# Alpha's transposes of the first nine units in the dense products' banks and one unit earlier

## The chip, the cores and the metric

The kernel runs on one core of a Trainium2 chip. The time is the device time of one execution in microseconds (us). Five engines each work through a queue of their own: TensorE (PE: matrix products, and transposes as products with an identity), VectorE (DVE), ScalarE (ACT), GpSimd (POOL) and SyncE (SP, which here issues the DMAs). An engine that meets an instruction whose input isn't ready waits, and all that is queued behind it waits too.

## What is computed

Gated linear attention, then a feed-forward layer on its output:

```python
state = np.zeros((B, H, D, D))                       # B=4, H=8, S=768, D=48
for t in range(S):
    state = alpha[:, :, t, :, None] * state + einsum('bhd,bhe->bhde', k[:, :, t], v[:, :, t])
    y[:, :, t] = einsum('bhd,bhde->bhe', q[:, :, t], state)
x = y.transpose(0, 2, 1, 3).reshape(B * S, H * D)    # 3072 x 384
h = x @ w_in                                         # 384 x 2048
out = np.maximum(0.01 * h, h) @ w_out                # 2048 x 384
```

## The kernel before

The 768 tokens of each batch are cut into chunks of 128, which gives 24 units (chunk t, batch b) of 128 tokens and 8 heads; heads go in four pairs p. Unit numbers run over the batches first, so units 0 to 3 are the first chunk of the four batches, 4 to 7 the second.

For a unit u the running products of alpha along the tokens turn the recurrence into products of matrices. `scans(u)` transposes alpha so that tokens lie along the free axis (four transposes on PE, L303) and then forms on DVE `pc`, the running product of each pair (four scans), and `rc`, its inverse counted backwards. `scaled_q` and `scaled_k` transpose q and k on PE and multiply them on DVE by `pc` and `rc`; the results are `qs` and `ks` (DVE writes them at L288, as it does `pc`, `rc` and the low half of y). Then:

- `scores(u)` multiplies `qs` by `ks` on PE (16 products into two banks, L540). `mask_scores` copies them on ACT to `sm` (L420) and zeroes a triangle on POOL (L422).
- `k_tokens(u)` transposes `ks` back (L437, tile `kt`), and ACT copies it to `ktok`.
- `past(u)` multiplies `qs` by the state into the bank of y, `values(u)` adds the masked scores times v to it, and `products(u)` makes the new part of the state, `kv`, from `ktok` and v. All three are L540 in the profile.
- `split(u)` writes y as a high half (ACT, L554) and a low half (DVE, tile `large`); `next_state(u)` adds `kv` to the state.

The first nine units (`AHEAD`) are issued by `attention(0, 9)`, in which unit u+1 is prepared while unit u is multiplied. Later units transpose on DVE and are spread among the dense products. The dense layer has 16 blocks f of 128 columns. The weights of a block come by DMA (tile `raw`) and `convert(f)` splits them into high and low parts on ACT (L260, L262, L269) and DVE (L266, L273, L275, L277, L280; tiles `bits`, `pw`, `w`). `ffn_in` multiplies into a bank `ph` (L714, nine products). ACT and DVE then form `t` (L719, L722), `gh` (L724) and `gl` (L728). `ffn_out` multiplies these by the second weights (L743). Two early `ffn_in` are placed behind `kt` of units 7 and 8 (`STARTS`).

PSUM has eight banks: two of tag `ph`, three of tag `a`, three of tag `b`. Within a tag the banks go round, so a new tile waits for the readers of the tile that had its bank. In the first nine units `bank()` gives `a` and `b` in turn. So alpha's, q's and k's transposes, both score banks, `kt`, y and `kv` all share one rotation. Unit 0's alpha goes half to `a` and half to `ph`.

Loads: q, k and alpha each have two buffers, with three more shared ones (`spare`), v has three. A load is issued on SP when the code asks for it, and waits for the buffer's last reader.

The order of an engine's instructions is not simply the order of the code. The compiler's scheduler places the instructions by its own estimate of times, within the dependencies, the pools' rotations and the explicit `behind(...)` marks, which hold an instruction behind a named earlier one. So a change in the first part moves rows on every engine. Lines on which the prediction turns:

```python
BEGIN = ("rc", 7), ("qs", 8), ("kt", 8)
STARTS = {62: ("kt", 7), 69: ("kt", 8)}
...
with behind("ks", u):
    convert(converted)
```

Of the kernel before, what the change touches and what calls it, by code (L numbers as in the profile page):

```python
# [10 lines left out]
F32 = mybir.dt.float32  # L11
# [13 lines left out]
def gated_linear_attn_ffn(ctx, tc, q, k, v, alpha, w_in, w_out, out):  # L25
    nc = tc.nc
    B, H, S, D = q.shape
    NT, DM = out.shape
    DF = w_in.shape[1]
    P = 128  # L30
# [3 lines left out]
    NP = H // 2  # L34
# [37 lines left out]

    halves = slice(0, HC), slice(HC, C)

    kinds = ["a", "b"]

    def bank(tag=None):
        if tag is None:
            tag = kinds[0]
            kinds.append(kinds.pop(0))  # L80
        return ps_x.tile([P, 512], F32, name=tag)

    def pieces(name, dtype, *shapes):
# [99 lines left out]
        if n < NV - 1:  # L183
            load_values(n)

    idle = ps_h.tile([P, 512], F32, name="ph")

    def keep_warm(n):

# [97 lines left out]

        return put(u >= AHEAD, "DVE", lambda: op(*args))  # L288

    def banks4():  # L290
        return bank().rearrange("r (p n) -> r p n", p=NP)

    def transposed(u, i, name, **kw):

        src = loaded(u, i)
        if u < AHEAD:
            ps = banks4()
            tiles = [ps[:, p, :] for p in range(NP)]
            if u == 0 and i == 0:
                other = ps_h.tile([P, 512], F32, name="ph").rearrange("r (p n) -> r p n", p=NP)  # L300
                tiles[NP // 2:] = [other[:, p, :] for p in range(NP // 2)]
            for p in range(NP):
                last = nc.tensor.transpose(  # L303
                    tiles[p], by_token(src)[:, 2 * p:2 * p + 2, :].rearrange("t h d -> t (h d)"), ident
                )
                if u == 0 and p % 2:
                    with tc.issue_after(last.ins):
                        keep_warm(WARM[2 * i + p // 2])
            return [ps, other] if u == 0 and i == 0 else ps
        t = atp.tile([P, NP, C], F32, name=name, **kw)  # L310
        src = src.rearrange("r (p n) -> r p n", p=NP)[:, :, 0:RUN]
        vector(
            u, nc.vector.transpose, t.rearrange("r p (j t) -> r p t j", t=T4),
            src.rearrange("r p (t d) -> r p t d", t=T4)[:, :, :, 0:32],
        )
        return t
# [114 lines left out]
    def k_tokens(u):  # L431
        if u >= AHEAD or units[u][0] < NC - 1:
            ks = live[u][2]
            kt = bank()
            for p in range(NP):
                with in_row() if u >= AHEAD else nullcontext():
                    made["kt", u] = nc.tensor.transpose(kt[:, p * BR:(p + 1) * BR], ks[0:BR, p, :], ident[0:BR, 0:BR])  # L437
            if row and u >= AHEAD:
                row[:] = [made["kt", u]]
            ktok = atp.tile([P, NP, BR], F32, name="ktok", bufs=1)  # L440
            made["sm", u] = nc.scalar.copy(ktok.rearrange("t p d -> t (p d)"), kt[:, 0:NP * BR])  # L441
            live[u][2:] = [ktok] if u < AHEAD else [ks, ktok]
# [10 lines left out]
    def past(u):  # L453

        tb, b = units[u]
        qs, W = live[u][1], state[b].rearrange("r p n -> r (p n)")
        y = banks4()
        ys[u] = [y]
        if tb:
            for q, s, lo, top, p, at in heads():  # L460
                c, m = p * BR + lo, D if top else HB
                yield y[at:at + m, 2 * q + s, :], W[0:BR, c:c + m], qs[0:BR, p, :], q == 0 and s == 0, False
# [33 lines left out]
    def products(u):  # L496

        tb, b = units[u]
        pe, qs, ktok = live[u][:3]
        V = vals_sb[u % NV]  # L500
        kv = None
        if tb < NC - 1:
            kv = bank()[:, 0:NP * D].rearrange("d (p e) -> d p e", p=NP)
            for p in range(NP):
                for s, lo, m in ((0, 0, HB), (1, HB, D)):
                    h = 2 * p + s
                    yield kv[lo:lo + m, p, :], ktok[:, p, lo:lo + m], V[:, h * D:(h + 1) * D], True, True
        load_values(u + NV)
        live[u] = pe, kv
# [99 lines left out]
    def every_step(steps):  # L609

        for _ in steps:
            pass

    def attention(first, last):

        for u in range(first - 1, last):
            new, old = u + 1 < last, u >= first
            if new:
                every_step(scans(u + 1))
                yield  # L620
            if old:
                multiply([scores(u)])
                yield
                mask_scores(u)
                yield
                k_tokens(u)
                sum_up(u)
                yield
            if new:
                every_step(scaled_q(u + 1))  # L630
                yield
                every_step(scaled_k(u + 1))
                yield
            if old:
                multiply([past(u), values(u), products(u)])
                split(u)
                yield
                next_state(u)
                if u % UPB == UPB - 1:
                    gather(u // UPB)  # L640
                    ready.add(u // UPB)
                yield
# [140 lines left out]
    for n, _ in enumerate(st):  # L783
# [12 lines left out]
        if n in STARTS:  # L796
            i, f = items[len(gs)][:2]
            with behind(*STARTS[n]):
                gs[len(gs)] = ffn_in(i, f)
    kinds[:] = "a"  # L800


    new = coming = None
# [197 lines left out]
```

## Time and profile before

| what | value |
|---|---|
| time, median of 3 runs | 511.39 us (510.27 to 513.04) |
| profiled execution, its own time | 510.39 us |
| span of that execution | 508.7 us |
| granted TensorE clock, mean | 0.997 |
| PE busy | 496.5 us (98%) |
| DVE busy | 371.3 us (73%) |
| ACT busy | 250.4 us (49%) |
| POOL busy | 68.7 us (13%) |
| DMA | 46.77 MB |

The profiled execution lies 1.00 us below the median of the runs, and 1.7 us of it are outside the span. Times in rows of the profile count from the span's start. In a row of the timeline stand the start, the duration, the engine, the line, what is written from what, the number of instructions, and in square brackets the engine's idle time just before, with what ended it. PE's matrix products overlap each other, so a row's duration is not the engine's pace.

### The profile page before, as it was taken

What the parts mean: (1) busy time and instruction counts of PE and PEld (TensorE: products, weight loads), DVE (VectorE), ACT (ScalarE), POOL (GpSimd) and SP (SyncE); (2) the same over time, 40 slices, a digit from 0 to 9 for tenths busy, and PEclk for the clock granted to TensorE, in tenths of its full rate; (3) what the DMA queues carried; (4) which work ended last, traced back from release to release, by engine and by line L of the source; (5) the groups of instructions that cost most, each with busy time, mean ns of one, the idle gap of its engine ahead of it and who ended that gap; (6) DMA issues with size and microseconds to landing.
All of it is one profiled execution on the core that took longest, in us unless ns stands there. A gap on an engine that the chain in (4) does not pass through costs nothing.

```text
span 508.7 us, 12195 instructions
## 1 busy us (share of the span) xinstructions
PE 496.5 (98%) x4906; PEld 479.1 (94%) x4906; DVE 371.3 (73%) x700; ACT 250.4 (49%) x524; POOL 68.7 (13%) x161
## 2 busy tenths in 40 slices
PE   8998999999999999999999999999999999999995
PEld 7786899999999999999999999999999999999995
DVE  7999899999999768777768578676768674333331
ACT  2666877767655444454444453354444543333331
POOL 5554500000001111101201211101101100000000
PEclk9999999999999999999999999999999999999998
DMA  9999986777204423524325323324321101001001
GB/s 145 167 184 182 220 179 181 208 170 204 36 1 118 139 62 73 120 60 120 73 59 115 102 60 90 70 68 118 78 57 40 50 2 24 1 0 48 1 0 52
DMA packets 92990, 46.77 MB, mean 92 GB/s; under 512 B 57856, under 2 KB 90112, under 8 KB 92928
## 3 DMA queue, kind: packets, MB, share of 16 engines
q1 hardware_dynamic: 92928, 45.93, 40.9%
q8 instruction: 40, 0.66, 0.6%
q14 instruction: 22, 0.18, 0.1%
HBM read 38.83 MB, written 4.72 MB: 86 GB/s over the span
## 4 chain that ended last, share of the span: by engine, by line
PE 80%; DVE 8%; DMA 6%; issue 2%; ACT 2%; SPq 2%; POOL 0%; DVEq 0%; ACTq 0%; POOLq 0%
PE ph L714 34%; PE b L743 32%; PE a L540 5%; PE a L743 3%; DMA raw<-in_moe_w_in_dram 3%; PE ph L540 2%; PE a L437 1%; DMA small<-in_alpha_dram 1%; DMA small<-in_v_dram 1%; DVE gl L728 1%; DVE ks L288 1%; DVE qs L288 1%; SPq L224 1%; DVE pw L277 1%; DVE t L722 1%
## 5 line engine op out<-in xcount | busy, mean ns | idle before, releaser
L714 PE MATMUL ph<-large,w 128*128 128x384 f32 x1152 | 225.1, 336 | 0.4 <-DVE w L280 0.2
L714 PEld LDWEIGHTS ph<-large,w 128*128 128x128 f32 x1152 | 200.5, 188 | 2.1 <-DVE t L722 1.1
L743 PE MATMUL b<-w,gh 128*128 128x384 f32 x672 | 168.3, 337 | 0.0
L722 DVE TENSOR_TENSOR t<-ph,t 128x384 f32<-128x384 f32 x128 | 70.4, 550 | 71.9 <-ACT t L719 71.8
L743 PEld LDWEIGHTS b<-w,gh 128*128 128x128 f32 x672 | 119.9, 188 | 1.3 <-ACT gh L724 0.2
L719 ACT ACTIVATE t<-ph 128x384 f32<-128x384 f32 x128 | 62.6, 489 | 111.5 <-PE ph L714 111.5
L724 ACT CAST gh<-t 128x384 fp32r<-128x384 f32 x128 | 65.8, 514 | 97.1 <-DVE t L722 97.0
L743 PE MATMUL b<-w,gl 128*128 128x384 f32 x336 | 108.1, 334 | 0.0
L728 DVE TENSOR_TENSOR gl<-t,gh 128x384 fp32r<-128x384 f32 x128 | 70.5, 551 | 31.1 <-ACT gh L724 31.1
L743 PEld LDWEIGHTS b<-w,gl 128*128 128x128 f32 x336 | 62.7, 188 | 0.0
L422 POOL TENSOR_SCALAR_AFFINE_SELECT sm<-sm 64x256 f32<-64x256 f32 (+1 forms) x48 | 26.2, 555 | 45.0 <-ACT sm L420 37.9
L288 DVE TENSOR_TENSOR_SCAN down<-e,small 128x511 f32<-128x511 f32 x15 | 19.3, 1287 | 6.4 <-DMA out_dram<-o 5.0
L535 POOL MEMSET small<- 128x1 f32 x15 | 1.5, 99 | 152.7 <-PE a L540 149.8
L540 PE MATMUL a<-qs,ks 48*64 48x64 f32 (+1 forms) x552 | 20.9, 228 | 0.2 <-ACT ktok L441 0.2
L288 DVE TENSOR_TENSOR_SCAN up<-e,small 128x128 f32<-128x128 f32 x60 | 20.4, 403 | 0.1
L743 PE MATMUL a<-w,gh 128*128 128x384 f32 x96 | 20.5, 334 | 0.0
L540 PEld LDWEIGHTS a<-qs,ks 48*64 48x64 f32 (+1 forms) x552 | 17.6, 142 | 1.8 <-issue 1.3
L358 POOL COPY small<-up 128x4 f32<-128x4 f32 x15 | 5.9, 395 | 94.6 <-DVE up L288 94.6
L262 ACT CAST signs<-raw 128x768 f16<-128x768 f32 x16 | 17.2, 1076 | 0.1
L743 PEld LDWEIGHTS a<-w,gh 128*128 128x128 f32 x96 | 17.0, 188 | 0.0
L288 DVE STREAM_TRANSPOSE e<-small 128x512 f32<-128x512 f32 x15 | 16.9, 1126 | 0.0
L420 ACT COPY sm<-a 128x256 f32<-128x256 f32 (+1 forms) x24 | 10.8, 452 | 11.7 <-PE b L540 11.7
(113 smaller groups left out, 612.4 us busy)
## 6 DMA issues: line engine op xcount, KB each, us to landing
raw<-in_moe_w_out_dram SPq DMA_DIRECT2D x16, 384.0 KB, 4.0
small<-in_v_dram SPq DMA_DIRECT2D x24, 192.0 KB, 3.9
raw<-in_moe_w_in_dram SPq DMA_DIRECT2D x32, 144.0 KB, 4.2
out_dram<-o SPq DMA_DIRECT2D x24, 192.0 KB, 2.7
small<-in_alpha_dram SPq DMA_DIRECT2D x32, 96.0 KB, 2.5
small<-in_q_dram SPq DMA_DIRECT2D x30, 96.0 KB, 2.2
small<-in_k_dram SPq DMA_DIRECT2D x30, 96.0 KB, 2.2
small<-in_alpha_dram SPq DMA_DIRECT2D x30, 80.0 KB, 2.2
```

The source lines that it names most:

```text
L262: put(ordered, "ACT", lambda: nc.scalar.copy(signs.bitcast(F16).rearrange("p (n w) -> p n w", w=2)[:, :, 1], top.bitcast(F32)))
L288: return put(u >= AHEAD, "DVE", lambda: op(*args))
L358: nc.gpsimd.tensor_copy(pe, pc[:, :, C - 1:C])
L420: made["sm", u] = nc.scalar.copy(sm[s], ss[s] if u < AHEAD else within(ss[s]))
L422: made["mask", u] = nc.gpsimd.affine_select(out=sm[s][part], in_=sm[s][part], compare_op=ALU.is_ge, fill=0.0, base=0, pattern=[[0, NP], [1 ...
L540: made["product",] = nc.tensor.matmul(out, weights, moving, start=start, stop=stop, skip_group_check=True)
L714: product = nc.tensor.matmul(ph, w_in_of(f, wn, g), xt[:, g, :], start=n == 0, stop=n == 3 * NG - 1)
L719: put(ordered, "ACT", lambda: nc.scalar.mul(t, ph, 0.01))
L722: put(ordered, "DVE", lambda: nc.vector.tensor_tensor(t, ph, t, ALU.max))
L724: put(ordered, "ACT", lambda: nc.scalar.copy(gh, t))
L728: made["gl", i, f] = put(ordered, "DVE", lambda: nc.vector.tensor_tensor(gl, t, gh.bitcast(F32), ALU.subtract))
L743: product = nc.tensor.matmul(po[j], gt[:, js], w_out_of(f, wn), start=f == 0 and n == 0, stop=f == NF - 1 and n == 2)
```

## The change

Alpha's transposes of the first nine units go to the banks of tag `ph`, which only the dense products (and, in unit 0, half of alpha and the idle products that keep PE busy at the start) used. The transposes of q and k and both score banks go to tag `a`; `kt`, y, `kv` and the idle products go to tag `b`. There is no rotation over both tags any more.

The transposing step of `scans` is taken out of its place and issued one unit earlier: `turn_alpha(u + 2)` stands right behind `scaled_k(u + 1)` and ahead of `past(u)`. For u = 4 and 5 two marks hold it there: alpha's transposes of unit u+2 behind the last transpose of k of unit u+1, and the first product of `past(u)` behind alpha's last transpose. The load of alpha is asked for as much earlier. The numbers of the lines shift: L303 becomes L300, L288 L285, L540 L538, L437 L435, L714 L728, L743 L757, L722 L736, L728 L742, L266 to L280 become L263 to L277.

```diff
--- before.py
+++ after.py
@@ -72,12 +72,9 @@
 
     halves = slice(0, HC), slice(HC, C)
 
-    kinds = ["a", "b"]
-
-    def bank(tag=None):
-        if tag is None:
-            tag = kinds[0]
-            kinds.append(kinds.pop(0))
+    def bank(tag="a"):
+        if tag == "ph":
+            return ps_h.tile([P, 512], F32, name=tag)
         return ps_x.tile([P, 512], F32, name=tag)
 
     def pieces(name, dtype, *shapes):
@@ -183,7 +180,7 @@
         if n < NV - 1:
             load_values(n)
 
-    idle = ps_h.tile([P, 512], F32, name="ph")
+    idle = bank("b")
 
     def keep_warm(n):
 
@@ -287,22 +284,23 @@
 
         return put(u >= AHEAD, "DVE", lambda: op(*args))
 
-    def banks4():
-        return bank().rearrange("r (p n) -> r p n", p=NP)
+    def banks4(tag="a"):
+        return bank(tag).rearrange("r (p n) -> r p n", p=NP)
 
     def transposed(u, i, name, **kw):
 
         src = loaded(u, i)
         if u < AHEAD:
-            ps = banks4()
+            ps = banks4("a" if i else "ph")
             tiles = [ps[:, p, :] for p in range(NP)]
             if u == 0 and i == 0:
-                other = ps_h.tile([P, 512], F32, name="ph").rearrange("r (p n) -> r p n", p=NP)
+                other = banks4("ph")
                 tiles[NP // 2:] = [other[:, p, :] for p in range(NP // 2)]
             for p in range(NP):
                 last = nc.tensor.transpose(
                     tiles[p], by_token(src)[:, 2 * p:2 * p + 2, :].rearrange("t h d -> t (h d)"), ident
                 )
+                made["turned", u, i] = last
                 if u == 0 and p % 2:
                     with tc.issue_after(last.ins):
                         keep_warm(WARM[2 * i + p // 2])
@@ -431,7 +429,7 @@
     def k_tokens(u):
         if u >= AHEAD or units[u][0] < NC - 1:
             ks = live[u][2]
-            kt = bank()
+            kt = bank("b" if u < AHEAD else "a")
             for p in range(NP):
                 with in_row() if u >= AHEAD else nullcontext():
                     made["kt", u] = nc.tensor.transpose(kt[:, p * BR:(p + 1) * BR], ks[0:BR, p, :], ident[0:BR, 0:BR])
@@ -454,7 +452,7 @@
 
         tb, b = units[u]
         qs, W = live[u][1], state[b].rearrange("r p n -> r (p n)")
-        y = banks4()
+        y = banks4("b")
         ys[u] = [y]
         if tb:
             for q, s, lo, top, p, at in heads():
@@ -500,7 +498,7 @@
         V = vals_sb[u % NV]
         kv = None
         if tb < NC - 1:
-            kv = bank()[:, 0:NP * D].rearrange("d (p e) -> d p e", p=NP)
+            kv = bank("b")[:, 0:NP * D].rearrange("d (p e) -> d p e", p=NP)
             for p in range(NP):
                 for s, lo, m in ((0, 0, HB), (1, HB, D)):
                     h = 2 * p + s
@@ -613,10 +611,19 @@
 
     def attention(first, last):
 
+        turned = {}
+
+        def turn_alpha(u):
+
+            if u < last:
+                turned[u] = scans(u)
+                next(turned[u])
+
+        turn_alpha(first)
         for u in range(first - 1, last):
             new, old = u + 1 < last, u >= first
             if new:
-                every_step(scans(u + 1))
+                every_step(turned.pop(u + 1))
                 yield
             if old:
                 multiply([scores(u)])
@@ -631,8 +638,15 @@
                 yield
                 every_step(scaled_k(u + 1))
                 yield
+            together = B <= u < last - 3
+            with behind("turned", u + 1, 2) if together else nullcontext():
+                turn_alpha(u + 2)
             if old:
-                multiply([past(u), values(u), products(u)])
+                group = past(u)
+                if together:
+                    with behind("turned", u + 2, 0):
+                        multiply([islice(group, 1)])
+                multiply([group, values(u), products(u)])
                 split(u)
                 yield
                 next_state(u)
@@ -797,7 +811,6 @@
             i, f = items[len(gs)][:2]
             with behind(*STARTS[n]):
                 gs[len(gs)] = ffn_in(i, f)
-    kinds[:] = "a"
 
 
     new = coming = None
```

What moves is seen at three places. The names are the program's tiles with the scheduler's numbers; `small_73` and `spare_74` are large tiles of many parts (q, k, alpha, v, the states), and the same number stands for the same piece of work in both kernels only for `ks`, `qs`, `pc`, `rc`, `sm`, `pw` and `bits`.

PE, end of unit 2's scores. Before: the keys of unit 2, then k (`a_391`) and q (`b_383`) of unit 3, two products of y, and alpha of unit 4 (`b_428`):

```order
L437 MATMUL a_374<-small_73,ks_311 128x112 x4
L303 MATMUL a_391<-small_73 128x128 x4
L303 MATMUL b_383<-small_73 128x128 x4
L540 MATMUL b_399<-sm_365,small_73 64x128
L540 MATMUL b_399<-sm_365,small_73 48x128
L303 MATMUL b_428<-small_73 128x128 x4
L540 MATMUL a_408<-small_73,ktok_379 64x48
```

Now: q (`a_383`), the keys, alpha of unit 4 (`ph_399`) and at once alpha of unit 5 (`ph_489`), then k (`a_391`):

```order
L300 MATMUL a_383<-small_73 128x128
L435 MATMUL b_374<-small_73,ks_311 128x112 x4
L300 MATMUL a_383<-small_73 128x128 x3
L300 MATMUL ph_399<-small_73 128x128 x4
L300 MATMUL ph_489<-small_73,spare_74 128x128 x4
L300 MATMUL a_391<-small_73 128x128 x4
L538 MATMUL b_404<-sm_365,small_73 64x128
L538 MATMUL b_404<-sm_365,small_73 48x128
```

Alpha of unit 4 stands ahead of k of unit 3 and y of unit 2, and alpha of unit 5 has come forward by a whole unit. Alpha of unit 3 likewise stands inside unit 0's y, alpha of unit 8 inside unit 5's.

DVE, the scaled keys of unit 7 (`ks_775`), which `scores(7)` on PE reads. `pw_732`, `bits_727` and `w0_726` are the conversion of weight block 0, `pc_811` the scans of unit 8. Before:

```order
L273 TENSOR_SCALAR pw_732<-bits_727 128x768
L288 TENSOR_TENSOR qs_768<-b_763,pc_715 128x512
L275 TENSOR_TENSOR bits_727<-bits_727,w0_726 128x768
L277 SCALAR_TENSOR_TENSOR pw_732<-raw_334,pw_732 128x768
L288 TENSOR_TENSOR ks_775<-a_770,rc_716 128x512
L288 SCALAR_TENSOR_TENSOR pc_811<-b_806,small_73 128x128 x4
L280 TENSOR_TENSOR w0_726<-pw_732,bits_727 128x768
L575 TENSOR_TENSOR small_73<-us2_424,a_794 112x192
```

Now:

```order
L270 TENSOR_SCALAR pw_732<-bits_727 128x768
L272 TENSOR_TENSOR bits_727<-bits_727,w0_726 128x768
L274 SCALAR_TENSOR_TENSOR pw_732<-raw_339,pw_732 128x768
L285 TENSOR_TENSOR qs_768<-a_763,pc_715 128x512
L285 SCALAR_TENSOR_TENSOR pc_811<-ph_777,small_73 128x128
L277 TENSOR_TENSOR w0_726<-pw_732,bits_727 128x768
L285 SCALAR_TENSOR_TENSOR pc_811<-ph_777,small_73 128x128 x3
L285 TENSOR_TENSOR ks_775<-a_770,rc_716 128x512
L573 TENSOR_TENSOR small_73<-us2_429,b_799 112x192
```

`ks_775` has moved behind the four scans of unit 8 and behind the last step of weight block 0.

DVE, the scaled keys of unit 8 (`ks_888`), which `scores(8)` reads. `t_858` and `gl_863` belong to the first `ffn_in`, `bits_873` to weight block 1. Before:

```order
L288 SCALAR_TENSOR_TENSOR rc_812<-b_806,small_73 128x511
L288 TENSOR_TENSOR ks_888<-a_883,rc_812 128x512
L288 TENSOR_TENSOR qs_870<-b_865,pc_811 128x512
L266 SCALAR_TENSOR_TENSOR bits_873<-raw_510,signs_120 128x768
L722 TENSOR_TENSOR t_858<-ph_848,t_858 128x384
L273 TENSOR_SCALAR pw_878<-bits_873 128x768
```

Now:

```order
L285 SCALAR_TENSOR_TENSOR rc_812<-ph_777,small_73 128x511
L736 TENSOR_TENSOR t_858<-ph_848,t_858 128x384
L285 TENSOR_TENSOR qs_870<-a_865,pc_811 128x512
L263 SCALAR_TENSOR_TENSOR bits_873<-raw_515,signs_120 128x768
L742 TENSOR_TENSOR gl_863<-t_858,gh_861 128x384
L285 TENSOR_TENSOR ks_888<-a_883,rc_812 128x512
L270 TENSOR_SCALAR pw_878<-bits_873 128x768
```

`ks_888` has moved behind `t_858`, `qs_870`, `bits_873` and `gl_863`.

On SP the loads of alpha of units 2 to 8 stand 1 to 10 places earlier among the loads, those of k one to three places later, the four pieces of the first weights of block 0 one place later; v of unit 6 is the 40th load in both orders, and from there on the loads agree.

## The prediction

> **What bounds the kernel now.** I first read busy time by stretches, since the average of a kernel in two parts tells little. The columns are the window, its length, then for PE, its weight loads, DVE, ACT and POOL the busy time and the instructions, the granted clock, the DMA share and the rate.
>
> ```profile
> core 0: us, PE busy (x) PEld busy (x) DVE busy (x) ACT busy (x) POOL busy (x), PEclk, DMA share, GB/s
> 40.00:50.00 10.00, 7.90 (x118) 6.48 (x118) 9.61 (x19) 6.04 (x12) 3.50 (x5) 1.00 1.20 192
> 50.00:60.00 10.00, 9.87 (x120) 8.88 (x120) 9.40 (x17) 8.97 (x20) 4.76 (x7) 1.00 0.98 198
> 60.00:70.00 10.00, 9.77 (x87) 8.61 (x81) 8.16 (x14) 7.51 (x14) 2.38 (x2) 1.00 0.92 227
> 70.00:110.00 40.00, 40.00 (x230) 39.81 (x231) 40.00 (x65) 29.69 (x47) 0.00 (x0) 1.00 0.75 186
> 131.00:151.00 20.00, 19.66 (x111) 18.76 (x110) 19.00 (x31) 11.33 (x20) 1.18 (x1) 1.00 0.00 0
> 151.00:300.00 149.00, 148.37 (x1728) 144.96 (x1728) 114.11 (x222) 68.74 (x160) 19.59 (x47) 1.00 0.37 93
> 300.00:480.00 180.00, 179.78 (x1848) 176.73 (x1847) 108.12 (x212) 74.24 (x166) 13.68 (x38) 1.00 0.18 46
> 480.00:508.70 28.70, 23.20 (x134) 22.88 (x133) 7.80 (x14) 7.00 (x14) 0.00 (x0) 0.94 0.07 23
> ```
>
> From 50 us on PE is the bound: it idles 0.13 in 50 to 60, nothing in 70 to 110, 0.63 in 151 to 300, 0.22 in 300 to 480. Whatever makes PE later after 50 us is paid unless one of these small idles takes it back. Only 40 to 50 us has a real hole, 2.10 us. The waits of the first 70 us (total, number, longest) say for what:
>
> ```profile
> PE b L540 <- DMA small<-in_v_dram: 1.6, 2, 1.4
> DVE pc L288 <- PE b L303: 2.6, 4, 1.0
> ```
>
> The second row is the wait that the moved instructions cause: four times DVE stands, 2.6 us in all, before it can scan alpha, because alpha's transposes are late on PE. PE itself waits little for DVE in these units. Its longest wait is a load. The timeline of PE around it, and one row from unit 1 that is needed below:
>
> ```profile
> 18.35 0.66 PE L303 MATMUL b<-small 128*128 128x128 f32 x4 [0.20 <-DMA small<-in_alpha_dram]
> ...
> 44.55 0.66 PE L303 MATMUL a<-small 128*128 128x128 f32 x4 [0.36 <-DVE small L575]
> ...
> 46.17 0.66 PE L303 MATMUL b<-small,spare 128*128 128x128 f32 x4
> 48.27 0.43 PE L540 MATMUL b<-sm,small 128*64 128x128 f32 x4 [1.44 <-DMA small<-in_v_dram]
> ...
> 49.72 0.37 PE L540 MATMUL a<-qs,ks 48*128 48x128 f32 x1
> ...
> 51.19 1.81 PE L714 MATMUL ph<-large,w 128*128 128x384 f32 x9
> ...
> 54.72 1.39 PE L540 MATMUL b<-sm,small 128*48 128x128 f32 x16
> ...
> 56.48 0.37 PE L540 MATMUL b<-qs,ks 48*128 48x128 f32 x1
> ...
> 61.26 0.43 PE L540 MATMUL a<-sm,small 128*64 128x128 f32 x4
> ...
> 61.96 0.87 PE L540 MATMUL a<-sm,small 128*64 128x128 f32 x12 [0.17 <-POOL sm L422]
> ```
>
> At 46.17 is alpha of unit 8. At 48.27 y of unit 6 starts, 1.44 us late, when v of unit 6 lands. `scores(7)` starts at 49.72, the first dense product at 51.19, `scores(8)` at 56.48, y of unit 8 at 61.26. So the part before 48.27 is paced by the loads, and the part behind it by PE and what feeds it. DVE in the same place, which is where the new order bites:
>
> ```profile
> 43.30 0.93 DVE L266 SCALAR_TENSOR_TENSOR bits<-raw,signs 128x768 int32<-128x768 int32 x1
> ...
> 47.03 1.38 DVE L277 SCALAR_TENSOR_TENSOR pw<-raw,pw 128x768 f32<-128x768 uint32 x1
> 48.33 0.68 DVE L288 TENSOR_TENSOR ks<-a,rc 128x512 f32<-128x512 f32 x1
> 48.93 1.35 DVE L288 TENSOR_TENSOR_SCAN pc<-b,small 128x128 f32<-128x128 f32 x4
> 50.21 0.93 DVE L280 TENSOR_TENSOR w<-pw,bits 128x768 fp32r<-128x768 f32 x1
> 51.06 0.34 DVE L575 TENSOR_TENSOR small<-us,a 112x192 f32<-112x192 f32 x1
> ...
> 53.53 0.69 DVE L288 TENSOR_TENSOR ks<-a,rc 128x512 f32<-128x512 f32 x1
> 54.14 0.68 DVE L288 TENSOR_TENSOR qs<-b,pc 128x512 f32<-128x512 f32 x1
> 54.74 1.25 DVE L266 SCALAR_TENSOR_TENSOR bits<-raw,signs 128x768 int32<-128x768 int32 x1
> 56.45 0.56 DVE L722 TENSOR_TENSOR t<-ph,t 128x384 f32<-128x384 f32 x1 [0.46 <-ACT t L719]
> 56.93 0.55 DVE L273 TENSOR_SCALAR pw<-bits 128x768 int32<-128x768 int32 x1
> ...
> 60.00 0.55 DVE L728 TENSOR_TENSOR gl<-t,gh 128x384 fp32r<-128x384 f32 x1
> ```
>
> The keys of unit 7 are made at 48.33 and those of unit 8 at 53.53, 0.7 and 2.3 us before PE asks for them.
>
> **The change, part by part.**
>
> Earlier transposes of alpha. The number of transposes and their durations stay (0.66 us for four). The 2.6 us of DVE's waits go. I cost this at nothing, gain or loss, because what is next is late for another reason: v of unit 6 is the 40th load before and after, the queue is full, and PE cannot pass 48.27 without it. If instead the loads did move up, the gain is bounded by the wait of 1.44 us on PE and by DVE's 2.6.
>
> Transposes that now wait for their load. Alpha of unit 3 ran at 18.35, just as it landed (0.20 us of wait). It is now the 11th load, not the 13th, but its transposes stand ahead of the rest of y of unit 0 and `scores(1)`, and alpha of unit 5 ahead of k of unit 3. PE will stand there, and behind it y and the scores of the unit. What covers this is the same wait for v of unit 6, 1.44 us, and work moved away from 46.17 (0.66 us), which leaves about 2.1 us of hole. I take nothing; the upper end is 1.0, if the two stalls add to more than the hole.
>
> Three banks a tag in place of one rotation of six. In these units the trace shows PE waiting for no reader of a bank beyond 0.4 us (44.55, a transpose behind a DVE read). I take 0, from -0.4 to +0.4.
>
> The keys of unit 7. They now stand behind the four scans of unit 8 and the last step of weight block 0. By the starts above, the scans take 50.21 - 48.93 = 1.28 and that step 51.06 - 50.21 = 0.85. The keys start at 48.33 + 1.28 + 0.85 = 50.46 and end at 51.1. PE, ready at 49.72, stands 1.4 us in front of `scores(7)`. DVE's sequence from 43.30 hangs on the first weights. Rows of SP, ACT, POOL and DVE that this and the next steps use:
>
> ```profile
> 33.57 3.70 SPq L224 DMA_DIRECT2D raw<-in_moe_w_in_dram  x4
> ...
> 40.84 0.92 ACT L260 ACTIVATE raw<-raw 128x768 f32<-128x768 f32 x1 [1.24 <-DMA raw<-in_moe_w_in_dram]
> ...
> 53.30 0.58 ACT L420 COPY sm<-a 128x512 f32<-128x512 f32 x1
> ...
> 57.48 0.56 ACT L724 CAST gh<-t 128x384 fp32r<-128x384 f32 x1
> ...
> 53.95 1.23 POOL L422 TENSOR_SCALAR_AFFINE_SELECT sm<-sm 128x512 f32<-128x512 f32 x2 [2.04 <-ACT sm L420]
> ...
> 58.60 3.31 POOL L422 TENSOR_SCALAR_AFFINE_SELECT sm<-sm 128x512 f32<-128x512 f32 x2 [2.24 <-ACT sm L420]
> ...
> 133.82 1.28 DVE L288 TENSOR_TENSOR_SCAN down<-e,small 128x511 f32<-128x511 f32 x1 [1.00 <-PE b L743]
> ```
>
> These weights are one place later on SP, and four issues took 3.70, so 0.9 a place: 1.4 to 2.3 us at `scores(7)`. Some 0.3 of it comes back at once: y and `kv` of unit 7 take 56.48 - 54.72 = 1.76 us in all, against 49.72 - 48.27 = 1.45 in unit 6, since ACT copies the scores of unit 7 only at 53.30. That copy doesn't move (scores that start at 51.1 to 52.0 end before 53.2).
>
> The keys of unit 8. They now stand behind `t`, `qs`, `bits` and `gl`. `t` starts at 56.45 as before, since ACT's queue ahead of it doesn't move and the dense product, 1.4 to 2.3 later than 51.19, still ends by 55.3. Then 0.48 (56.93 - 56.45), 0.60 for `qs` (54.74 - 54.14), 0.95 to 1.25 for `bits` (rows at 43.30 and 54.74), 0.55 for `gl` (`gh`, done at 58.04, is no hindrance) and 0.6 to 0.7 for the keys: they are ready at 59.6 to 60.0. `scores(8)` starts then, 3.1 to 3.5 us behind 56.48; this contains the lateness from unit 7. I take 3.3.
>
> y of unit 8. It took 61.96 with a pause for the mask, which ran 3.31 us there against 1.23 for unit 7. With the short mask 0.3 to 0.4 us come back; with the long one nothing. The row alone leaves both; I take 0.3 back, so PE is 3.0 behind at 66 us.
>
> By the Trainium skill, SBUF — State Buffer, section Who interferes with whom, a VectorE instruction with two SBUF inputs and a GpSimd one that reads SBUF block each other for whole instructions. The trace agrees: the 3.31 us run beside such rows (`gl` at 60.00, from `t` and `gh`), the 1.23 us start beside reads of PSUM. By it the mask of unit 8 stays long, as L272 and L274 then follow on DVE, and the sum would be 3.3 here.
>
> What is given back. In 131 to 151, 111 products ran in 20.00 us against 230 in 40.00 at 70 to 110, so 4 too few, at 0.174 us each 0.70 us. DVE stood 1.00 us there for a product at 133.82, and was late with the next weights. Then come 0.63 idle to 300 and 0.22 to 480. A PE that is later meets feeders that are ready, so up to 0.70 + 0.63 + 0.22 = 1.55 us; the lower end is 0, if the feeders are as late. I take all of it, because each is a wait for an engine that has slack otherwise (DVE 108 of 180, ACT 74). The last stretch keeps its order.
>
> Sum: 0 + 0 + 0 + 3.3 - 0.3 - 1.55 = +1.45. Against the profiled execution that is 510.39 + 1.45 = 511.84, and since that execution lies 1.00 below the median of the runs (511.39), I forecast 512.84, in short 512.8.
>
> **The rivals.** A difference of 0.5%, 2.56 us, is about what a measurement of this kernel tells from none.
>
> 1. Nothing is given back, and the mask stays long: 3.5 us at `scores(8)`, 514.9, or 515.9 with the uncovered 1.0 of the transposes. For it: DVE and PE are both full from 70 to 110, so DVE may be as late as PE, and then stands for PE again at 133.82. Against it: DVE has idles of its own in 60 to 70 (8.16 of 10). It decides from 2.56 net, so if less than 0.9 of 3.5 comes back.
>
> 2. Faster: the loads move up. SP waits for a buffer before it issues; with alpha transposed earlier the buffers come free earlier, v of unit 6 lands earlier and the hole of 1.44 and part of DVE's 2.6 go, while the first weights, `t` and `gl` move up by the same and cover the new order of the keys. That gives 1.44 to 2.6 below the time before: 508.8 to 509.9. Against it: DMA shares of 1.20 and 0.98 in 40 to 60 show a queue that is full, not one that waits. It decides if v of unit 6 lands before 46.8, where PE is done with the row at 46.17, and the keys move up as well.
>
> 3. No change: the order written for the engines differs, but the keys are ready as before because DVE, rid of its waits, runs ahead. The chain would then give 511.4, from -0.5 to +0.5. Against it: at 43.30 DVE started on weights that had just come, so it cannot run ahead there.
>
> 4. The clock drops at the hole before y of unit 6. It is 1.44 us now; with alpha of unit 8 taken from 46.17 it is about 2.1. In the last stretch, where PE idles most, the granted clock was 0.94 over 28.7 us, 1.7 us of clock. Such a loss on top gives 512.8 + 1.7 = 514.5. Against it: 40 to 50 us, with 2.10 us idle, kept 1.00.
>
> The Trainium skill, TensorE: Matmul & The Clock Gate, section HAM oscillation — how this bites in real kernels, states that idle gaps above some 3.4 us throttle the clock. The trace agrees so far as its longest quoted gap left the clock at 1.00; by that rule 2.1 us do no harm, which is why this rival has little.
>
> **How the numbers follow.** The forecast (two new waits on PE, a part of them given back, +0.5 to +2.5) has 0.50; rival 1 has 0.25, rival 2 0.10, rival 3 0.10, rival 4 0.05. Rivals 1 and 4 end partly within 2.56, so slower by over 0.5% gets 0.28, faster 0.10, and 0.62 remain for no difference that can be told. The range for 8 in 10 goes from 510.2 (half of rival 2 left out) to 515.1 (the upper end of rival 1 left out); the forecast's own is 511.9 to 513.9.
>
> **What would show it.** Right: PE with a wait of 1 to 2.5 us for DVE's `ks` ahead of each of the two last `scores`; DVE without its four waits for alpha; y of unit 6 still released by v near 48.3; in 131 to 151 more than 111 products. The step of the keys is wrong if `scores(8)` starts before 58 us, the step of the loads if v of unit 6 lands elsewhere than 47.5 to 49, and the part given back if PE's lateness at 66 us is still whole at 480. The prediction as a whole fails if PE stalls for alpha of units 3 and 5 outgrow the hole, or if a bank in a tag of three is waited for.

## The result, and the profile after

The changed kernel took 514.41 us (median of 13 executions, 512.52 to 517.50), the kernel before 512.03 (13 executions, 509.74 to 513.04). The ratio is 1.0065, with a 95% interval from 1.0047 to 1.0083: slower by 0.65%, or 3.3 us. The profiled execution took 514.78 us, its span 513.1, at a mean clock of 0.990. The stretches again, in the columns shown before:

```profile
40.00:50.00 10.00, 9.05 (x133) 7.61 (x131) 9.79 (x18) 7.89 (x17) 5.14 (x9) 1.00 1.17 205
50.00:60.00 10.00, 7.62 (x45) 6.92 (x46) 5.73 (x13) 5.69 (x11) 2.08 (x5) 0.66 1.01 198
60.00:70.00 10.00, 10.00 (x130) 8.94 (x129) 8.54 (x14) 7.86 (x15) 3.24 (x3) 1.00 0.82 193
131.00:151.00 20.00, 20.00 (x117) 20.00 (x117) 19.76 (x33) 13.17 (x22) 1.21 (x1) 1.00 0.22 32
151.00:300.00 149.00, 148.00 (x1724) 144.12 (x1723) 113.74 (x218) 68.04 (x158) 18.53 (x47) 1.00 0.36 89
300.00:480.00 180.00, 179.81 (x1850) 176.87 (x1849) 110.93 (x218) 75.58 (x170) 14.71 (x38) 1.00 0.20 50
```

The hole of 40 to 50 us is half closed (idle 0.95, before 2.10). In 50 to 60 stands what the kernel before did not have: PE idles 2.38 us, and the granted clock is 0.66; 45 instructions ran where 120 had. PE's longest waits behind the first products, and its timeline there:

```profile
PE a L538 <- DVE ks L285: 3.2, 1, 3.2
PE ph L300 <- DMA spare<-in_alpha_dram: 1.7, 1, 1.7
...
PE ph L300 <- DMA small<-in_alpha_dram: 1.0, 1, 1.0
```

```profile
47.21 0.43 PE L538 MATMUL b<-sm,small 128*64 128x128 f32 x4
...
52.38 2.08 PE L538 MATMUL a<-qs,ks 48*128 48x128 f32 x16 [3.18 <-DVE ks L285]
54.39 1.01 PE L435 MATMUL b<-small,ks 112*128 112x112 f32 x4
55.08 3.23 PE L728 MATMUL ph<-large,w 128*128 128x384 f32 x9
...
62.15 1.16 PE L538 MATMUL a<-qs,ks 48*128 48x128 f32 x16
...
66.92 0.43 PE L538 MATMUL b<-sm,small 128*64 128x128 f32 x4
```

y of unit 6 starts at 47.21 without a wait for v. Then PE stands 3.18 us for the keys of unit 7. What follows runs at half speed: `scores(7)` takes 2.08 us (the scores of unit 8 take 1.16), the nine dense products 3.23 (before 1.81). The clock in windows of a few microseconds shows the fall, which begins while PE still stands, and its end:

```profile
51.00:52.00 1.00, 0.00 (x0) 0.00 (x0) 1.00 (x4) 0.97 (x2) 0.12 (x1) 0.97 0.88 177
52.00:55.00 3.00, 2.62 (x19) 2.40 (x20) 2.59 (x6) 0.99 (x2) 0.26 (x2) 0.50 1.10 181
55.00:58.00 3.00, 3.00 (x12) 3.00 (x11) 0.00 (x0) 2.29 (x7) 1.70 (x3) 0.50 1.08 225
58.00:59.00 1.00, 1.00 (x7) 0.70 (x6) 0.14 (x1) 0.49 (x1) 0.00 (x0) 0.61 1.10 214
```

y of unit 8 starts at 66.92 instead of 61.26, so PE is 5.66 us late there. It did not stand ahead of `scores(8)`: PE came to them later than their keys. The spans differ by 513.1 - 508.7 = 4.4, so 1.26 was given back later. DVE and POOL at the same place:

```profile
42.70 1.28 DVE L285 TENSOR_TENSOR_SCAN rc<-ph,small 128x511 f32<-128x511 f32 x1
43.90 0.93 DVE L263 SCALAR_TENSOR_TENSOR bits<-raw,signs 128x768 int32<-128x768 int32 x1
...
46.26 1.44 DVE L272 TENSOR_TENSOR bits<-bits,w 128x768 f32<-128x768 f32 x1
...
51.67 0.66 DVE L285 TENSOR_TENSOR ks<-a,rc 128x512 f32<-128x512 f32 x1
...
58.87 0.56 DVE L736 TENSOR_TENSOR t<-ph,t 128x384 f32<-128x384 f32 x1 [4.27 <-ACT t L733]
...
61.27 0.69 DVE L285 TENSOR_TENSOR ks<-a,rc 128x512 f32<-128x512 f32 x1
...
64.06 2.77 POOL L420 TENSOR_SCALAR_AFFINE_SELECT sm<-sm 128x512 f32<-128x512 f32 x2 [7.15 <-ACT sm L418]
```

DVE goes from the scan `rc` of unit 7 straight to `bits`. The keys of unit 7 end at 52.3. DVE itself then waits 4.27 us, by way of ACT, for the dense product that PE runs late and slowly.

### The profile page after: what moved, and what is told of

Read it like the earlier page. It is cut to its first block, busy times and chain, and to the rows that moved or that the text cites. A ratio compares the mean times of both kernels' runs of the same rounds, so it can differ in the third digit from the quotient of the medians.

```text
span 513.1 us, 12212 instructions
## 1 busy us (share of the span) xinstructions
PE 497.5 (97%) x4906; PEld 482.6 (94%) x4906; DVE 371.9 (72%) x700; ACT 250.9 (49%) x524; POOL 66.8 (13%) x161
## 4 chain that ended last, share of the span: by engine, by line
PE 85%; DVE 8%; DMA 2%; ACT 2%; issue 1%; SPq 0%; DVEq 0%; POOL 0%; ACTq 0%
PE ph L728 36%; PE b L757 33%; PE a L538 6%; PE a L757 3%; PE b L538 2%; PE ph L538 2%; DVE ks L285 1%; PE a L435 1%; DMA small<-in_alpha_dram 1%; PE a L300 1%; DVE qs L285 1%; PE b L188 1%; DMA spare<-in_alpha_dram 1%; DVE gl L742 1%; DVE w L277 1%
## 5 line engine op out<-in xcount | busy, mean ns | idle before, releaser
L728 PE MATMUL ph<-large,w 128*128 128x384 f32 x1152 | 226.1, 337 | 0.2 <-DMA large<-large 0.2
L728 PEld LDWEIGHTS ph<-large,w 128*128 128x128 f32 x1152 | 201.9, 189 | 1.1 <-issue 0.5
L757 PE MATMUL b<-w,gh 128*128 128x384 f32 x672 | 168.3, 337 | 0.0
L736 DVE TENSOR_TENSOR t<-ph,t 128x384 f32<-128x384 f32 x128 | 70.5, 551 | 76.2 <-ACT t L733 76.1
L757 PEld LDWEIGHTS b<-w,gh 128*128 128x128 f32 x672 | 120.0, 188 | 1.1
L757 PE MATMUL b<-w,gl 128*128 128x384 f32 x336 | 108.1, 334 | 0.0
L742 DVE TENSOR_TENSOR gl<-t,gh 128x384 fp32r<-128x384 f32 x128 | 70.6, 552 | 31.0 <-ACT gh L738 31.0
L757 PEld LDWEIGHTS b<-w,gl 128*128 128x128 f32 x336 | 62.7, 188 | 0.0
L538 PE MATMUL a<-qs,ks 48*64 48x64 f32 (+1 forms) x624 | 21.6, 238 | 3.4 <-DVE ks L285 3.2
L538 PEld LDWEIGHTS a<-qs,ks 48*64 48x64 f32 (+1 forms) x624 | 18.3, 150 | 4.9 <-DVE ks L285 3.3
L285 DVE TENSOR_TENSOR_SCAN down<-e,small 128x511 f32<-128x511 f32 x15 | 19.3, 1287 | 4.6 <-DMA out_dram<-o 4.1
L418 ACT COPY sm<-a 128x512 f32<-128x512 f32 (+1 forms) x33 | 15.2, 488 | 14.9 <-PE a L538 14.9
L285 DVE TENSOR_TENSOR_SCAN up<-e,small 128x128 f32<-128x128 f32 x60 | 20.4, 403 | 0.1
L757 PE MATMUL a<-w,gh 128*128 128x384 f32 x96 | 20.2, 334 | 0.0
L757 PEld LDWEIGHTS a<-w,gh 128*128 128x128 f32 x96 | 17.0, 188 | 0.0
L285 DVE STREAM_TRANSPOSE e<-small 128x512 f32<-128x512 f32 x15 | 16.9, 1127 | 0.0
```

The lines of the kernel that those rows point to most:

```text
L418: made["sm", u] = nc.scalar.copy(sm[s], ss[s] if u < AHEAD else within(ss[s]))
L538: made["product",] = nc.tensor.matmul(out, weights, moving, start=start, stop=stop, skip_group_check=True)
L728: product = nc.tensor.matmul(ph, w_in_of(f, wn, g), xt[:, g, :], start=n == 0, stop=n == 3 * NG - 1)
L736: put(ordered, "DVE", lambda: nc.vector.tensor_tensor(t, ph, t, ALU.max))
L742: made["gl", i, f] = put(ordered, "DVE", lambda: nc.vector.tensor_tensor(gl, t, gh.bitcast(F32), ALU.subtract))
L757: product = nc.tensor.matmul(po[j], gt[:, js], w_out_of(f, wn), start=f == 0 and n == 0, stop=f == NF - 1 and n == 2)
```

## The experiments

The theories, as the expectations name them. A: the keys come late in DVE's queue, PE stands for them, and after a long hole its clock falls. B: only the wait counts, the clock is a side matter. C: PE's stalls for the loads of alpha of units 3 and 5, or the banks in threes, are the cost. Where an edit says "order", it adds dependencies that only order two instructions of one engine, written as (later, earlier); all else is left to the scheduler. Ratios are to the kernel before, run on the same chip, with the 95% interval.

### The two halves of the change

The banks alone: the kernel before with the new tags and no `turn_alpha`.

> The kernel before with the new banks alone; alpha's transposes stay in their place. The keys of unit 7 stand behind unit 8's four scans but ahead of weight block 0's last step, those of unit 8 behind t and bits. Theory A: a hole of 1 to 1.5 us, too short for the clock, scores(8) 2 to 3 us late: 512.5 to 514.5 by the late keys, granted clock 1.00. Theory B: the same, 512.5 to 514.5. Theory C with the stalls as the cause: no stall for alpha here, so 512.0 as before; with the banks as the cause: 514.4.

514.56 us, ratio 1.0054 (1.0033 to 1.0075). The early transposes alone: `turn_alpha` and the two marks in the old rotation.

> The kernel before with alpha's transposes one unit earlier, in the old rotation over six banks. Here the keys of unit 7 stand ahead of unit 8's scans and of weight block 0's last step. Theories A and B: no long hole, granted clock 1.00 in 50 to 60, time 510.5 to 512.5, as before or a little under. Theory C with the stalls for alpha of units 3 and 5 as the cause: 514 to 515.

510.53 us, ratio 0.9977 (0.9964 to 0.9990). So the banks bring the loss, and the early transposes by themselves bring a small gain. The banks alone let the scheduler write an order much like the changed kernel's: the keys of unit 7 behind unit 8's scans, alpha of units 3 and 5 far forward. Its PE:

```profile
52.14 1.20 PE L537 MATMUL a<-qs,ks 48*128 48x128 f32 x16 [2.40 <-DVE ks L285]
```

In the early transposes alone the keys kept their place. One execution took 514.7 us, and it is the profiled one. There the hole is at y of unit 6, and the clock behind it falls:

```profile
48.46 0.43 PE L541 MATMUL a<-sm,small 128*64 128x128 f32 x4 [2.50 <-DMA small<-in_v_dram]
50.00:60.00 10.00, 10.00 (x99) 9.37 (x98) 6.33 (x12) 7.07 (x14) 2.66 (x5) 0.68 0.95 202
```

### The keys of unit 7 put back

```diff
+ order: (first scan of unit 8, ks of unit 7), (w of block 0, ks of unit 7)
```

> The changed kernel with the keys of unit 7 held ahead of unit 8's scans and of the last step of weight block 0 on DVE; the alpha transposes stay early. Theories A and B: scores(7) starts at about 50.2 instead of 52.4, the hole on PE shrinks from 3.2 to about 1 us, granted clock 1.00 in 50 to 60, time 510.0 to 512.0, at or below the kernel before. Theory C: 514 to 515, since the stalls for alpha and the banks stay.

509.83 us, 0.9964 (0.9944 to 0.9984). A second run on another chip:

> The changed kernel with unit 7's keys in place, as measured at 509.83 (0.9964 of the kernel before). If the keys are the cause: 509 to 511 again, below the kernel before. If the first eight executions were lucky: 511 to 512.

510.99 us, 0.9992 (0.9970 to 1.0013). PE in the second:

```profile
50.59 1.16 PE L538 MATMUL a<-qs,ks 48*128 48x128 f32 x16 [1.06 <-DVE ks L285]
...
57.68 1.16 PE L538 MATMUL a<-qs,ks 48*128 48x128 f32 x16 [0.31 <-DVE ks L285]
...
62.45 0.43 PE L538 MATMUL b<-sm,small 128*64 128x128 f32 x4
```

The hole is 1.06 us instead of 3.18, and y of unit 8 starts 4.47 us earlier than in the changed kernel. The stalls for alpha (1.38 and 1.83 us here) are still there. With banks and stalls left as they were, this order takes the changed kernel's loss away. It is not the keys of unit 7 alone: around them the scheduler also put `qs` and `bits` ahead of `t`, and the keys of unit 8 (at 56.95) ahead of `gl` (58.01). Whether a gain over the kernel before remains is not settled: the first run says so, the second does not.

The reverse, the old kernel with the keys of unit 7 held back:

```diff
+ order: (ks of unit 7, w of block 0), (ks of unit 7, last scan of unit 8)
```

> The kernel before, old banks and old alpha, with one thing: the keys of unit 7 held on DVE behind unit 8's four scans and the last step of weight block 0 (the scheduler then also puts those of unit 8 behind t and bits). Theory A: PE waits 1.4 us for the keys ahead of scores(7) and up to 2 ahead of scores(8); 512.5 to 514.5, which is the loss of the change without the change. Theory C (banks or early alpha themselves cost): 511.4, as the kernel before.

512.96 us, 1.0020 (1.0000 to 1.0040). The time lies in the range I gave, but by the ratio the loss is 1.0 us, not the 3.3 of the change: the late keys alone bring back about a third of it. The profiled execution, the slowest of twelve at 515.60, shows the same picture as the changed kernel, on the old banks:

```profile
52.98 0.55 PE L540 MATMUL a<-qs,ks 48*128 48x128 f32 x1 [2.76 <-DVE ks L288]
50.00:60.00 10.00, 7.24 (x46) 6.56 (x43) 5.68 (x13) 5.77 (x11) 3.12 (x6) 0.66 0.99 208
```

### The clock apart from the wait

Idle products in the hole keep PE busy and change nothing that the keys wait for. The first try put 18 into the changed kernel.

```diff
                 multiply([group, values(u), products(u)])
+                if u == AHEAD - 3:
+                    cover = bank("b")
+                    with behind("product",):
+                        for _ in range(18):
+                            made["cover",] = nc.tensor.matmul(cover[:, 0:C], seed[:, 0, :], seed[:, 1, :], start=True, stop=True)
...
```

Further lines hold `scores(7)` behind the idle products, and `qs` and `ks` of unit 8 behind `t` and `gl`, where the changed kernel has them.

> The changed kernel with 18 idle products of 128x128 on PE between the new state of unit 6 and scores(7), about 2 us of work in the hole of 3.18 us; the keys of unit 7 are as late as before, so scores(7) starts at 52.4 either way. Theory A (the hole trips the clock, and the half clock from 52 to 59 us is most of the loss): granted clock 1.00 in 50 to 60 us, y of unit 8 near 63.5 instead of 66.9, time 511.0 to 513.0, with the executions closer together than 512.5 to 517.5. Theory B (the lateness of the keys is the loss, the clock a side matter): time 514 to 515, as the changed kernel. Theory C (stalls of 1.0 and 1.7 us for alpha of units 3 and 5, and banks in threes): 514 to 515.

514.51 us, 1.0054 (1.0035 to 1.0073). A product takes 0.23 us, twice what I had reckoned, so 18 of them ran until 54.8, 1.0 us past the keys (done at 53.8). The other 1.4 us by which `scores(7)` is later than in the changed kernel were lost before: the clock of the profiled execution fell from 24.9 to 28.3 us. So this run cannot price the clock at the hole. With eight:

> The changed kernel with 8 idle products between unit 6's state and scores(7): at the 0.234 us each that the 18 took they fill 1.9 of the 3.18 us, so they end before the keys of unit 7 come. Theory A (half clock after the long hole is a part of the loss): scores(7) released by the keys as in the changed kernel, granted clock 1.00 in 50 to 60 us, no execution of 516 to 517.5; median 1 to 2.5 us below the changed kernel, 512.0 to 513.5. Theory B (only the wait counts): 514.0 to 514.8. What is left above 511.4 is the wait itself.

513.74 us, 1.0037 (1.0017 to 1.0057), none above 515.25. Its PE:

```profile
49.14 2.05 PE L655 MATMUL b<-small 128*128 128x128 f32 x16
52.39 1.16 PE L538 MATMUL a<-qs,ks 48*128 48x128 f32 x16 [1.20 <-DVE ks L285]
...
59.93 1.16 PE L538 MATMUL a<-qs,ks 48*128 48x128 f32 x16 [0.64 <-DVE ks L285]
...
64.69 0.43 PE L538 MATMUL b<-sm,small 128*64 128x128 f32 x4
50.00:60.00 10.00, 8.16 (x98) 7.18 (x96) 8.03 (x16) 6.62 (x13) 2.07 (x5) 1.00 1.00 215
```

`scores(7)` starts at the same 52.4 as in the changed kernel and now takes 1.16 us, and y of unit 8 starts at 64.69 instead of 66.92. So at y of unit 8 the half clock is 2.23 us of the 5.66 in these two profiles, and the late keys are the other 3.43. At the end the spans differ by only 0.4 (513.1 and 512.7), because this execution stood later for a cause of its own, the DMA that moves rows of y within `large`:

```profile
220.62 1.83 PE L734 MATMUL ph<-large,w 128*128 128x384 f32 x9 [1.33 <-DMA large<-large]
```

Over all executions the ratios differ by 0.0028, 1.4 us, and the intervals overlap. The median lies a little above what theory A gave.

The same in the old kernel with late keys, five idle products:

> The kernel before with unit 7's keys held back (512.96, where PE stood 2.76 us in the profile and the clock fell to 0.66 in 50 to 60 us), plus five idle products (1.2 us) on PE around the end of y of unit 6, in the hole. Theory A: the clock stays at 1.00 in 50 to 60 and what is left is the wait: 511.5 to 512.5. Rival (the clock a side matter): 513.0, unchanged.

512.04 us, 1.0009 (0.9993 to 1.0024), none above 512.98, where 515.6 had been reached without them. The clock in 50 to 60 was 1.00. The ratios differ by 0.0011, 0.6 us, and the intervals overlap here too. And eight in the hole ahead of y of unit 6 in the early transposes alone:

> The kernel before with early alpha in the old banks (510.53; 509.2 to 511.9 and one execution of 514.7 at a clock of 0.991), plus eight idle products (1.9 us) on PE in the hole before y of unit 6. If the fall of the clock comes from the hole: no execution under a clock of 0.996 and none above 512.5; median 509.5 to 511, as the load sets the end of the hole anyway. Rival (the idle products delay what follows them): 511 to 512.5.

510.66 us, 0.9987 (0.9968 to 1.0006): no fall in the profile, but the median is that of the kernel without them, one execution was at 513.1, and another still had a mean clock of 0.993. Its worst case is better by 1.6 us, on one execution each.

### What did not come out

Putting the keys back does not mend the banks alone:

> The new banks alone, with the keys of unit 7 held ahead of unit 8's scans and of weight block 0's last step. Theory A: the 3.2 us that the banks alone lose against the kernel before come from these keys, so 510.0 to 512.0. Theory C (three banks of a kind make PE wait): 514 to 515, as the banks alone.

514.93 us, 1.0056 (1.0035 to 1.0077). Theory A in its simple form falls here. The profiled execution, the slowest of six, had two falls of the clock, in 25 to 29 and in 52 to 56 us, and behind 131 us PE stood twice for `large<-large`, 2.2 us in all. I then held alpha back too, first in the changed kernel with the keys in place.

```diff
+ order: (alpha of unit 3, k of unit 2), (alpha of unit 5, k of unit 4)   [PE, transposes]
```

> The changed kernel with the keys of unit 7 in place and, besides, alpha's transposes of units 3 and 5 held behind k's of units 2 and 4, so that PE no longer stands 1.4 and 1.8 us for their loads in units 0 and 2. Theory A with the clock: the half clock that the profile of the kernel with the keys in place shows after the stall at 23 to 25 us (0.83 in 20 to 30) goes too, in the executions that have it; median 508.3 to 509.5 and no execution above 511. Rival: those stalls are covered by the loads, and the time is that of the keys alone, 509.8.

513.49 us, 1.0037 (1.0022 to 1.0052). My edit made a new hole: alpha of unit 8 uses the buffer of unit 5, so its load came later, but its transposes kept their early place.

```profile
44.13 0.87 PE L300 MATMUL ph<-small,spare 128*128 128x128 f32 x3 [4.64 <-DMA spare<-in_alpha_dram]
40.00:50.00 10.00, 5.87 (x60) 5.32 (x60) 4.76 (x9) 3.73 (x6) 0.51 (x3) 0.66 1.26 200
```

With unit 8 held behind k of unit 7 as well:

> The kernel before this one in the list without its idle products; instead alpha of units 3, 5 and 8 is held behind k of units 2, 4 and 7 (with units 3 and 5 alone held, the load of alpha of unit 8 came late and PE stood 4.64 us for it, 513.49). Theory A with the clock: no stall for a load of alpha above 0.5 us, clock 0.998 or more in all executions, 508 to 510. Rival (holding alpha back itself costs, not the stall for unit 8's load): 513 to 514.

510.23 us, 0.9981 (0.9956 to 1.0005): that hole is gone, and so is its cost, 2.9 us by the ratios. But two of twelve executions still took 514 us at a clock of 0.99. The same three orders in the banks alone:

> The new banks alone, with unit 7's keys in place and alpha of units 3, 5 and 8 held behind k of units 2, 4 and 7. The banks alone let the scheduler put alpha of units 3 and 5 as early as the whole change does, and lost 3.2 us; with the keys alone in place they still lost 3.7. Theory A, widened (the cost of the banks is the order that they allow: late keys, and stalls for alpha's loads that halve the clock): 510 to 512. Theory C (three banks of a kind cost by themselves): 514 to 515.

515.21 us, 1.0072 (1.0044 to 1.0099). Its profiled execution, at 513.50, had no fall of the clock while PE worked, so the loss there is waits. PE also stood for the keys of unit 8:

```profile
58.77 1.16 PE L539 MATMUL a<-qs,ks 48*128 48x128 f32 x16 [1.57 <-DVE ks L285]
```

So I put those in place too (ahead of `t`, `qs` and `bits`), with the banks alone and with the whole change.

> The new banks alone with the keys of units 7 and 8 both in place on DVE. If the order of the keys is all that the banks cost: 510.5 to 512.0. If stalls for alpha's loads in units 0 and 2 and the half clock after them cost it: 513 to 515, as with unit 7's keys alone.

512.63 us, 1.0018 (1.0003 to 1.0032). With both keys in place two thirds of the banks' loss are gone; 0.9 us of it is left unexplained. The split is rough, since PE's order moved here as in the next run.

> The changed kernel with the keys of unit 7 in place, and those of unit 8 ahead of t, qs and bits as in the kernel before. With unit 7's alone PE waited 0.31 us for unit 8's. If the keys of unit 8 hardly matter: 509.3 to 510.2, as with unit 7's alone (509.83). If my step that priced them at 1.8 us of wait was right once unit 7's are in place: 507.5 to 508.5.

512.06 us, 1.0022 (1.0007 to 1.0038), slower than with unit 7's keys alone, which neither expectation gave. The edit moved PE's order: the second dense product now stands ahead of `scores(8)`, and y of unit 8 waits for the mask.

```profile
59.12 1.16 PE L538 MATMUL a<-qs,ks 48*128 48x128 f32 x16
...
64.89 0.43 PE L538 MATMUL b<-sm,small 128*64 128x128 f32 x4 [0.75 <-POOL sm L420]
```

So this run doesn't price the keys of unit 8. The last two put idle products ahead of alpha of unit 5 (and ahead of y of unit 6 in the second):

> The kernel with the new banks, early alpha and unit 7's keys in place (509.83, four of eight executions with a mean clock of 0.999 or more at 507.9 to 509.5, four with 0.995 to 0.997 at 510.2 to 512.1), plus six idle products on PE (1.4 us) in unit 2 ahead of alpha's transposes of unit 5, where PE stood 1.77 us for their load and the clock fell to half right after. Theory A with the clock: no execution below a clock of 0.998, all of them at 507.5 to 509.8, median 508.5. Rival (the clock there costs nothing because the loads pace that part): 509.8, unchanged.

510.73 us, 0.9983 (0.9962 to 1.0003), one execution at 514.4. Theory A gave 508.5. In the profile the stall of unit 5 is filled, PE stands 1.74 us for v of unit 6 instead, and the clock falls there.

> As keys78, with five idle products ahead of alpha's transposes of unit 5 and five ahead of y of unit 6, the two places where PE stands for loads. If the falls of the clock after those holes are what spreads the executions (508 to 512, some at 514): all executions at 0.998 or more, 507.5 to 510, median under 509.5. If idle products delay what follows as much as they save: 510 to 511.

512.14 us, 1.0015 (0.9999 to 1.0031), with a fall after the stall of 1.38 us for alpha of unit 3, which I had left. In both profiles the fall stood at the next hole instead, and the medians gained nothing.

## Why the prediction was wrong

I forecast 512.8 us, 1.45 above the kernel before, within 0.5% of it as the likeliest case, and it is slower by 3.3 us or 0.65%. The time lies in the range; the case I thought likeliest does not hold.

- **The place** was right. PE stood for the keys of unit 7 in front of `scores(7)`, and most of that lateness was still there at the end. The second wait that I named, ahead of `scores(8)`, did not come in this execution.
- **The step on unit 7's keys** was mis-sized, 1.4 to 2.3 us against 3.18. The keys started at 51.67, not at 50.46 to 51.4. I had tied DVE's start to the place of the first weights, here and against rival 3. But in both kernels DVE came to `bits` straight from `rc`, and ACT had taken the first weights up 2.5 us earlier (40.84 and 41.40):

```profile
42.10 1.28 DVE L288 TENSOR_TENSOR_SCAN rc<-b,small 128x511 f32<-128x511 f32 x1
```

This scan was 2.08 us late for unit 5, behind PE's stalls for alpha, and 0.60 still for unit 7. L272 then took 1.44 us where L275 had taken 1.02, both beside the mask of unit 6. And PE came sooner, at 49.2, because it did not wait for v of unit 6.
- **The step on earlier transposes** said that PE cannot pass 48.27 without v of unit 6. The load was issued at the same time, 41.54 against 41.58, but landed 4.7 us later instead of 6.5, so at 46.2, before PE asked at 47.21; in the early transposes alone it took 7.0. Rival 2 had named 46.8 as its sign, but the keys did not move up with it. I took one execution's landing for a fixed time.
- **The step on unit 8's keys** came out in sum: without the half clock PE was 3.43 us behind at y of unit 8, where I had 3.3 and 3.0 after the mask. I took 0.3 back for a short mask; it ran 2.77 us, and y of unit 8 starts when it ends. Here the Trainium skill, SBUF — State Buffer, section Who interferes with whom, had it right: with two-input VectorE rows beside it the mask stays long.
- **What is given back** was 1.26 us in the profile, against 1.55. 117 products ran in 131 to 151 us (111 before), as I had reckoned, but from 151 to 300 PE idled 1.00 us, not less than the 0.63 before. With 3.43 that leaves 2.2 us for an execution without a fallen clock, an estimate; the kernel with eight idle products lost 1.9 by its ratio. So some 0.7 us of what I missed are the mask and the give-back.
- **The clock** is the step that failed: I put it at nothing in the sum. Rival 4 had the mechanism at the wrong hole, 2.1 us at y of unit 6, with a chance of 0.05; I had taken a hole of that size as harmless. Behind the hole of 3.18 us the clock was 0.50 for 6.8 us. This costs 2.23 us at y of unit 8 in the pair of profiles, and 1.4 on average by the ratios of the kernels with and without idle products. That rival 4's 514.5 lies next to the measured 514.41 is luck: its price of 1.7 us came from the last stretch, where the clock fell only after PE's last product, at no cost:

```profile
505.00:508.70 3.70, 0.00 (x0) 0.00 (x0) 0.00 (x0) 0.00 (x0) 0.00 (x0) 0.56 0.09 27
```

By the Trainium skill, TensorE: Matmul & The Clock Gate, section HAM oscillation — how this bites in real kernels, gaps above some 3.4 us throttle; here holes of 1.1 to 3.2 us did, so the measurement decides against the rule as I used it.
- **No gain from DVE's waits** held, but not all of the 2.6 us went: unit 1's wait stayed (1.04, now 1.25), those of units 3, 6 and 7, 1.56 us, are gone. The early transposes alone, in which they are gone too, gained 0.23%.

Not settled: what the last 0.9 us of the banks are, why the banks with unit 7's keys alone in place gain nothing, on what the waits for `large<-large` depend, and why the scheduler puts the keys behind the scans. That alpha in free banks looks ready sooner to it is only argued.

## What to carry to other kernels

Giving a transpose its own banks changed more here than the waits for banks: the scheduler wrote another order on PE and on DVE. So read from the new order what now stands ahead of each instruction that PE waits for, and price the hole from both ends, when the feeder is done and when PE arrives. A hole of a microsecond or more on TensorE may cost twice, once as a wait and again as half clock behind it; and a fix that fills or closes one hole has to be checked against the next.

## What the hardware showed that I had not expected

The clock fell to 0.50 for about 3.4 us (seven times) or about 6.8 us (five times), besides the fall behind PE's last product that every profile has. At holes of 2.40 us and more it fell in every profile (2.40, 2.50, 2.76, 3.18 and 4.64 us). Of twelve holes of 1.73 to 1.87 us it fell at five, so the length of the hole does not decide there. One program shows both: with unit 7's keys in place it fell after 1.77 us in the first run, and not after 1.83 in the second:

```profile
25.11 0.90 PE L300 MATMUL ph<-small,spare 128*128 128x128 f32 x4 [1.77 <-DMA spare<-in_alpha_dram]
20.00:30.00 10.00, 8.07 (x91) 6.84 (x88) 7.43 (x18) 4.74 (x13) 4.47 (x11) 0.83 1.09 170
...
51.91 1.16 PE L538 MATMUL a<-qs,ks 48*128 48x128 f32 x16 [1.06 <-DVE ks L285]
```

```profile
25.37 0.63 PE L300 MATMUL ph<-small,spare 128*128 128x128 f32 x4 [1.83 <-DVE pc L285]
20.00:30.00 10.00, 7.97 (x105) 6.77 (x102) 8.08 (x18) 5.79 (x15) 4.79 (x13) 1.00 1.14 170
```

This is the cleanest price of a fall. The first execution is 0.26 us ahead at alpha of unit 5 and 1.32 behind at `scores(7)` (51.91 against 50.59), with the same waits in between, so 3.4 us at half clock cost it 1.6 us there.

So the same program spreads over several microseconds: the changed kernel's three executions with a mean clock under 0.990 took 516.7 to 517.5 us, its two at 0.997 took 512.5 and 513.8. The waits for `large<-large` behind 131 us, from nothing to 2.2 us in a profile, spread them too.
